# SwiGLU feed-forward on one core: a transposing load issued by ScalarE, half-chunk ups in the head, and seven casts placed behind the tail copies

## The chip, the core and the metric

The kernel runs on one core of a Trainium2 chip. The metric is the device time in microseconds of one execution; 116.36 us is the median of three runs of the kernel before. The engines are TensorE (PE in the profile; PEld is its weight load), VectorE (DVE), ScalarE (ACT), GpSimd (POOL) and SyncE (SP). SP does no arithmetic, it issues DMAs; ACT can issue DMAs too, on a queue of its own (the profile calls SP's queue q1 and ACT's q10). Each engine runs its own instructions in a fixed order and waits on semaphores.

## What is computed

```python
B, S, D, F = 1, 2048, 512, 1376          # bf16
g = silu(x @ w_gate)                     # [S, F]
u = x @ w_up                             # [S, F]
return (g * u) @ w_down                  # [S, D]
```

## The kernel before

**Tiling.** Tokens are cut into four chunks of 512 (c = 0 to 3), F into ten tiles of 128 (ft = 0 to 9) and a remainder of 96, D into four blocks of 128 (dk). x is kept transposed in `xT_sb` (D on the partitions), so that `w_sb` gives the stationary operand and x the moving one, and PSUM holds h transposed. PSUM has eight banks of 128x512 fp32.

**Two ways of multiplying.** Most of the gate and up work, and part of the down projection, is done two tiles by two chunks at a time with seven products in place of eight. VectorE and GpSimd form the sums of blocks that this needs (S1 to S4 and a cast A22 of the stationary side, T1 to T4 and a cast B22 of the moving side), PE multiplies them in fp32r. The rest, F tiles 0 to 5 of chunk 0 and some tiles of chunk 1, is done plainly: `classic` (L455) does a gate group and an up group of eight matmuls each (`gu_emit`, L406: for each dk two matmuls of 64 columns of F side by side), then ACT takes the silu and DVE multiplies (`classic_out`, L450). This plain work comes first, while weights and sums arrive.

**The order of the work.** Every operation is added to a `Plan` (L30) with the keys it reads and writes, an assumed duration, and a priority. PE and SP keep the order in which operations are added. For ACT, DVE and POOL `schedule` (L58) picks, by assumed times, whatever can start first, and by priority among equals (lower numbers first; the casts here have 9, the copies out of PSUM 0 to 2). The order so found is then fixed in the program. `after=` adds a dependency on given operations. So where an operation stands in the queue of ACT or DVE follows from assumed times, and when it runs follows from semaphores.

**Loads (L253 to L319).** All are issued by SP, in this order: `xn`, tokens 0 to 255 as they lie in memory (L282); `wg0`, gate weights of F tiles 0 and 1 (L289); `x0b`, tokens 256 to 511 by a transposing DMA (L290, issued at L279); `wu0`, up weights of F tiles 0 and 1 (L291); then weights `wg2`, `wu2`, `wg4`, `wu4` (L292), the transposing load `x1` of chunk 1 (L294), `wg6`, `wu6`, `wg8`, `wu8`, `wut`, `x2`, `x3`, the down weights `wd` and small pieces. Each weight load of two F tiles is 256 KB, `x0b` is 256 KB, each of `x1` to `x3` 512 KB.

**The head (L340 to L391, L670 to L680).** PE runs warming matmuls, then transposes tokens 0 to 255 itself; DVE and ACT copy the four dk blocks out of PSUM into `xT_sb` (`x0a`, L391; ACT has dk 1 and 3). On ACT stands ahead of these copies only a small silu of constants (L342), which makes it load its table. Then PE does F tiles 0 and 1 of chunk 0: gates on tokens 0 to 255 (sixteen matmuls of 256 columns), gates on tokens 256 to 511 (sixteen more, they need `x0b`), ups on all 512 tokens (sixteen matmuls of 512 columns, they need `wu0` and `x0b`).

**The start of the down projection (L933 to L980).** PE does plain output tiles (`body`, L699, into banks 4, 5, 0 and 1), and between them two blocks of `tails` (L711): the contribution of the 96 remaining F rows, in matmuls of 32 rows of which four run side by side. After the first block ACT copies banks 2, 3, 6 and 7 to `ts_sb` (`keep_tails`, L741); ACT also copies the finished output tiles to `o_sb` (`out_tile`, L693). After the second block ACT copies the same banks to `sg_sb`. Then come two seven-product units (`DownUnit`, L828): `a` with X, Y, W in banks 1, 3, 2 and `b` with 6, 3, 7. The first product of `a`, `p1` (L881, matmuls at L850), writes bank 1, so it must wait until `out_tile` of tile N3+1 has copied that bank. `keep` (L857, on DVE) reads bank 1 after each of `p1`, `p6` and `p7`.

`down_sums` (L756) adds the sums for those units: S1, S2 on POOL, T1 to T4, S3 and S4 on DVE, and on ACT seven casts (L818 to L821, issued from L527): two of 128x640 for A22 and five of 128x512 for B22, with priority 9 and behind T1 (`late`). A22 is read first by `a.p4` (L903), B22 by `a.p3` (L907).

Of the kernel before, what the change touches and what calls it, by code (L numbers as in the profile page):

```python
# [4 lines left out]
ACT = mybir.ActivationFunctionType  # L5
# [9 lines left out]
A_BUSY, A_LAG = 485, 180  # L15
# [152 lines left out]
def bass_standalone__swiglu_ffn__prompt_kernel(nc, x, w_gate, w_up, w_down, out):  # L168
    _, S, D = x.shape
    F = w_gate.shape[1]  # L170
    P = 128
# [26 lines left out]
    with ExitStack() as es:  # L198
# [53 lines left out]

        landed = 2700  # L253

        def load(name, emit, writes, busy, lag):
            nonlocal landed
            landed += lag
            i = take(homes[name] if name in homes else rest[0])
            plan.add("S", emit, writes=writes, busy=busy, lag=1800, dma=(i, 16)).land = landed + (2500 if landed > 10000 else 0)

        slabs = [(0, 2), (2, 4), (4, 6), (6, 8), (8, NFF + 1)]
        slab_of = {ft: a for a, b in slabs for ft in range(a, b)}
# [1 line left out]
        def load_w(name, src, m, c0, f0, f1):  # L264
            load(
                name,
                lambda e: e.dma_start(
                    w_sb[:, :, m, c0:c0 + f1 - f0], src[:, f0:f1].rearrange("(k p) f -> p k f", p=P)
                ),
                [name], 600, 3.2 * (f1 - f0),  # L270
            )
# [2 lines left out]
            load_w(f"wg{a}", w_gate, 0, a * P, a * P, min(b * P, F))  # L274
            load_w(f"wu{a}", w_up, 1, a * P, a * P, min(b * P, F - 32))

        def load_x(name, t0, t1):
            load(
                name, lambda e: e.dma_start_transpose(xT_sb[:, :, t0:t1], xf[t0:t1, :]), [name], 1500, 4.6 * (t1 - t0)  # L279
            )  # L280

        load(  # L282
            "xn",
            lambda e: e.dma_start(
# [1 line left out]
            ),  # L286
            ["xn"], 500, 770,
        )
        load_w("wg0", w_gate, 0, 0, 0, slabs[0][1] * P)  # L289
        load_x("x0b", HT, SC)  # L290
        load_w("wu0", w_up, 1, 0, 0, slabs[0][1] * P)  # L291
        for a, b in slabs[1:3]:  # L292
            load_slab(a, b)
        load_x("x1", SC, 2 * SC)  # L294
        for a, b in slabs[3:]:
            load_slab(a, b)
        load_w("wut", w_up, 0, F, F - 32, F)
# [41 lines left out]

        plan.add("G", lambda e: e.iota(diag[:, :], pattern=[[-1, P]], base=0, channel_multiplier=1), (), ["diag"], 300, 100, 0)  # L340
        plan.add("D", lambda e: e.tensor_single_scalar(ident[:, :], diag[:, :], 0.0, ALU.is_equal), ["diag"], ["ident"], 200, 100, 0)
        plan.add("A", lambda e: e.activation(adummy[:, 0:4], zero_c, ACT.Silu), (), ["adummy"], 1500, 100, 0)  # L342

        def pe(emit, reads, writes, n, step=PE_STEP, after=()):
            return plan.add("P", emit, reads, writes, int(n * step), PE_LAG, dma=None, after=after)
# [60 lines left out]
        def gu_emit(m, ft, c, b, dks, n0, n1):  # L406
            def emit(e):
                for dk in dks:
                    for h in (0, HC):
                        ins = e.matmul(  # L410
                            psum[h:h + HC, b, n0:n1], lhsT=w_sb[:, dk, m, ft * P + h:ft * P + h + HC],
                            rhs=xT_sb[:, dk, c * SC + n0:c * SC + n1], start=(dk == 0), stop=(dk == KD - 1),
                            tile_position=(0, h),
                        )
                return ins
            return emit
# [255 lines left out]
        for dk in range(KD):  # L672
            for ft, b in ((0, g0), (1, g1)):
                pe(gu_emit(0, ft, 0, b, [dk], 0, HT), [("x0a", dk), wkey[0]], [("b", b)], 0.5)
        for ft, b in ((0, g0), (1, g1)):
            pe(gu_emit(0, ft, 0, b, range(KD), HT, SC), ["x0b", wkey[0]], [("b", b)], 2)
        for ft, b in ((0, u0), (1, u1)):
            gu_group(1, ft, 0, b)
        classic_out(0, 0, g0, u0)
        classic_out(1, 0, g1, u1)  # L680

# [59 lines left out]
        def keep_tails(members, name, tiles):  # L741
            for c, (kind, i, b, start) in enumerate(members):
                if kind == "T":
                    t, k = ring(name, tiles)
                    tail_at[i, c] = t, k
                    copy_op("A", t, bank(b), [("b", b)], [k], 2)

        def before(keys):

# [6 lines left out]
        def down_sums(pool_after):  # L756

            flat = lambda s: ss_sb[:, s, :, :, :, :].rearrange("p n m k c -> p (n m k c)")
            NJ = NFF // 2
            HALF = NJ * 2 * P  # L760
            used = lambda s: before([("ss", s, n, m) for n in W_SUM.values() for m in range(2)] + [("ss", s, n, m) for n in W_SUM for m in range(2)])
            slots = {n: (slot_of[U_ORDER[1][1]], i) for i, n in enumerate(("S1", "S2"))}
            slots |= {n: (slot_of[U_ORDER[1][2]], i) for i, n in enumerate(("S3", "S4"))}
            slots["A22"] = slot_of[U_ORDER[1][4]], 0
            wview = wd_sb[:, :, :].rearrange("p (j a) (q e c) -> p a e j q c", a=2, e=2, c=P)
            hview_ = h0_sb[:, :, :].rearrange("p (j a) (c t) -> p a c j t", a=2, c=2)
            ds, dt = {}, {}
            for n, (s, i) in slots.items():
                ds[n] = flat(s)[:, i * HALF:(i + 1) * HALF].rearrange("p (j q c) -> p j q c", j=NJ, q=2)
            tt1 = tt_sb[1][:, :, :, :].rearrange("p n k c -> p (n k c)")  # L770
            tile = lambda a, i: a[:, i * NJ * SC:(i + 1) * NJ * SC].rearrange("p (j t) -> p j t", j=NJ)
            dt["T1"], dt["T2"], dt["T3"], dt["T4"] = tile(tt1, 0), tile(tt1, 1), th_sb[:, 0, :, :], th_sb[:, 1, :, :]
            dt["B22"] = tile(flat(slot_of[U_ORDER[1][3]]), 0)
            free = {"T1": before([("tt", 1, n, k) for n in X_SUM.values() for k in range(KH)])}
            free["T2"] = free["T1"]
            free["T3"] = free["T4"] = before([f"w{g}{a}" for g in "gu" for a, _ in slabs] + ["wut"])
            free["B22"] = used(slot_of[U_ORDER[1][3]])

            def s_sum(n, eng, after):
# [12 lines left out]

            def t_sum(n):
                for j0, j1 in ((0, 1), (3, 5), (1, 3)):
                    at = lambda n: dt[n][:, j0:j1, :]
                    rd = lambda n: at(n).bitcast(FP32)
                    B11, B12, B21, B22 = (hview_[:, k, c, j0:j1, :] for k in range(2) for c in range(2))
                    a, b, of_ = {
                        "T1": (B12, B11, ()), "T2": (B22, rd("T1"), ["T1"]),
                        "T3": (B22, B12, ()), "T4": (B21, rd("T2"), ["T2"]),  # L800
                    }[n]
                    t_ops[n] = tt_op(
                        "D", at(n), a, b, ALU.subtract,
                        [("h", ft, c) for ft in range(2 * j0, 2 * j1) for c in range(2)] + [("dt", o, j) for o in of_ for j in range(j0, j1)],
                        [("dt", n, j) for j in range(j0, j1)], 9, 1150 if j1 - j0 == 2 else D_BUSY, free[n],
                    )

            t_ops = {}
            s_sum("S1", "G", pool_after)
            s_sum("S2", "G", pool_after)  # L810
            t_sum("T1")
            t_sum("T2")
            t_sum("T3")
            s_sum("S3", "D", [t_ops["T3"]])
            t_sum("T4")
            s_sum("S4", "D", [t_ops["T4"]])
            late = [t_ops["T1"]]
            for q in range(2):  # L818
                cast_op("A", ds["A22"][:, :, q, :], wview[:, 1, 1, :, q, :], ["wd"], [("ds", "A22", q)], 9, 600, used(slots["A22"][0]) + late)
            for j in range(NJ):  # L820
                cast_op("A", dt["B22"][:, j, :], hview_[:, 1, 1, j, :], [("h", 2 * j + 1, 1)], [("dt", "B22", j)], 9, A_BUSY, free["B22"] + late)  # L821
            return ds, dt

        xflat = xT_sb[:, :, :].rearrange("p k t -> p (k t)")
        oT_sb = xflat[:, 0:KD * S // 2].rearrange("p (d c t) -> p d c t", d=KD, c=2)
# [104 lines left out]
            )  # L930
            copy_op("D", o_all[:, ob, c0:c1], psum[:, b, 0:c1 - c0], [("b", b)], [("o", t, c0)], 1)

        def down(ds, dt):  # L933
            N2, N3 = NST // 2, NST // 2 + TPC
            x_used = before([f"x{c}" for c in range(1, NSC)] + x_keys(0))
            for n0, n1 in ((0, NFF - 2), (NFF - 2, NFF)):
# [13 lines left out]
            first = [("T", 2, 2, True), ("T", 2, 3, True), ("N", N2 + 2, 4, True), ("N", N3 + 2, 5, True)]  # L950
            second = [("T", 3, 6, True), ("T", 3, 7, True), ("N", N2 + 3, 0, True)]
            tails([first, second])
            for members in (first, second):
                keep_tails(members, "sg", sg_sb)
            a = DownUnit(0, (1, 3, 2), ds, dt, x_used)
            b = DownUnit(1, (6, 3, 7), ds, dt, x_used)
            a.p1()
# [63 lines left out]
        for n in range(len(units)):  # L1021
# [12 lines left out]
            unit.p3()  # L1034
            unit.p4()
            unit = after
        ds, dt = down_sums(pool_last)
        down(ds, dt)

        plan.schedule()  # L1040
        plan.emit(engines, sems)
# [30 lines left out]
```

## Time and profile before

| | us |
|---|---|
| median of three runs (116.28 to 116.48) | 116.36 |
| the profiled execution | 116.42 |
| its span, first to last instruction | 115.1 |
| PE busy in the span | 111.0 |
| DVE, ACT, POOL busy | 76.4, 60.6, 59.9 |
| granted TensorE clock | 1.0 |

The profiled execution's own time is 1.3 us longer than its span: that is what lies around the instructions. All positions in time below are microseconds from the start of the span. Times of matmuls in the trace overlap, since their ends are modelled: the distance between starts is the rate.

### The profile page before, as it was taken

Reading aid. Unit: us, or ns where it says so; the run is one execution under the profiler, and the core shown is the slowest. Engines: PE = TensorE matmul, PEld = TensorE weight load, DVE = VectorE, ACT = ScalarE, POOL = GpSimd, SP = SyncE. Lnnn points to the kernel's source line nnn. Section 1 sums busy time; section 2 is a strip of 40 time slices with the busy share of each in tenths; the row PEclk is TensorE's granted clock in tenths of the full one; section 3 lists DMA queues with packets and bytes.
Section 4 is the critical chain, followed back from the end, with each engine's and each line's share of the span. In section 5 each row is a group of like instructions: output and inputs, shape, how many; then the busy total and the mean of one; then the engine's idle time right before and its main releaser. Section 6 shows DMA issues by size and latency. Waiting matters only on the chain.

```text
span 115.1 us, 1806 instructions
## 1 busy us (share of the span) xinstructions
PE 111.0 (96%) x662; PEld 66.9 (58%) x670; DVE 76.4 (66%) x112; ACT 60.6 (53%) x116; POOL 59.9 (52%) x75
## 2 busy tenths in 40 slices
PE   7989999999999999999999999999998999999993
PEld 2655555554567667685858676553443656866452
DVE  0113599766659394866849393799999977486423
ACT  5344276599756767878676767630799600000000
POOL 1475000599999999799999999980000000000000
DMA  3999899991000000000000000000022002327966
GB/s 95 261 292 252 216 282 267 251 354 31 0 0 0 0 3 3 0 6 0 3 0 0 0 0 0 6 0 0 0 91 80 11 0 46 51 46 181 200 193 201
DMA packets 22776, 9.84 MB, mean 86 GB/s; under 512 B 12816, under 2 KB 22640, under 8 KB 22768
## 3 DMA queue, kind: packets, MB, share of 16 engines
q1 hardware_dynamic: 20624, 8.69, 30.3%
q10 hardware_dynamic: 2144, 1.05, 3.2%
q8 instruction: 5, 0.08, 0.3%
q14 instruction: 3, 0.02, 0.1%
HBM read 4.75 MB, written 2.10 MB: 60 GB/s over the span
## 4 chain that ended last, share of the span: by engine, by line
PE 79%; DVE 7%; ACT 6%; DMA 3%; SPq 2%; issue 1%; DVEq 0%
PE psum L593 26%; PE psum L410 12%; PE psum L605 10%; PE psum L838 10%; PE psum L703 7%; PE psum L421 5%; PE psum L850 4%; DMA w_sb<-in_w_up_dram 3%; DVE tt_sb L336 3%; PE psum L474 3%; ACT ss_sb L527 3%; ACT o_sb L324 2%; ACT ts_sb L324 2%; PE psum L500 1%; SPq L279 1%; DVE h_sb L336 1%
## 5 line engine op out<-in xcount | busy, mean ns | idle before, releaser
L593 PE MATMUL psum<-tt_sb,ss_sb 128*128 128x512 f32 x140 | 35.3, 404 | 0.0
L593 PEld LDWEIGHTS psum<-tt_sb,ss_sb 128*128 128x128 f32 x140 | 26.3, 188 | 6.4
L336 DVE TENSOR_TENSOR ts_sb<-r_sb,psum 128x512 f32<-128x512 f32 x28 | 17.9, 682 | 12.4 <-ACT r_sb L324 12.4
L336 DVE TENSOR_TENSOR h_sb<-sg_sb,psum 128x512 bf16<-128x512 f32 x26 | 17.8, 683 | 8.6 <-PE psum L410 7.0
L331 ACT ACTIVATE sg_sb<-psum 128x512 f32<-128x512 f32 x26 | 15.5, 598 | 14.3 <-PE psum L410 7.8
L336 POOL TENSOR_TENSOR ss_sb<-w_sb 128x256 fp32r<-128x256 bf16 x20 | 13.1, 675 | 15.3 <-DVE tt_sb L336 11.1
L336 POOL TENSOR_TENSOR h_sb<-sg_sb,ts_sb 128x512 bf16<-128x512 f32 x14 | 18.4, 1314 | 1.7 <-ACT sg_sb L331 1.5
L703 PE MATMUL psum<-wd_sb,h_sb 128*128 128x512 bf16 (+2 forms) x97 | 18.0, 335 | 0.2
L324 ACT ACTIVATE r_sb<-psum 128x512 f32<-128x512 f32 x28 | 15.2, 595 | 5.7 <-PE psum L593 5.7
L410 PE MATMUL psum<-xT_sb,w_sb 128*64 128x512 bf16 (+1 forms) x160 | 16.1, 360 | 0.4 <-DMA w_sb<-in_w_up_dram 0.4
L703 PEld LDWEIGHTS psum<-wd_sb,h_sb 128*128 128x128 bf16 x100 | 8.3, 98 | 9.2 <-issue 1.0
L410 PEld LDWEIGHTS psum<-xT_sb,w_sb 128*64 128x64 bf16 x160 | 9.0, 111 | 7.3 <-DMA w_sb<-in_w_up_dram 0.7
L605 PE MATMUL psum<-xT_sb,w_sb 128*128 128x512 bf16 x52 | 12.6, 380 | 0.4 <-issue 0.2
L331 ACT ACTIVATE sg_sb<-ts_sb 128x512 f32<-128x512 f32 x14 | 8.9, 634 | 1.6 <-DVE ts_sb L336 1.6
L605 PEld LDWEIGHTS psum<-xT_sb,w_sb 128*128 128x128 bf16 x56 | 4.8, 98 | 7.0 <-issue 2.3
L336 POOL TENSOR_TENSOR ss_sb<-w_sb,ss_sb 128x256 fp32r<-128x256 bf16 x10 | 6.6, 683 | 0.0
L336 POOL TENSOR_TENSOR ss_sb<-ss_sb,w_sb 128x256 fp32r<-128x256 f32 x10 | 6.6, 676 | 0.0
L325 DVE CAST o_sb<-psum 128x512 bf16<-128x512 f32 (+2 forms) x6 | 2.9, 512 | 4.2 <-PE psum L703 3.1
L421 PE MATMUL psum<-xT_sb,w_sb 128*128 128x512 bf16 x24 | 5.7, 379 | 0.0
L838 PE MATMUL psum<-tt_sb,ss_sb 128*128 128x512 f32 x20 | 5.6, 417 | 0.0
L325 DVE COPY psum<-psum 128x512 f32<-128x512 f32 x7 | 4.9, 700 | 0.9 <-ACT sgy_sb L331 0.3
L838 PE MATMUL psum<-th_sb,ss_sb 128*128 128x512 f32 x20 | 5.5, 414 | 0.0
(71 smaller groups left out, 124.7 us busy)
## 6 DMA issues: line engine op xcount, KB each, us to landing
wd_sb<-in_w_down_dram SPq DMA_DIRECT2D x1, 1280.0 KB, 8.3
w_sb<-in_w_gate_dram SPq DMA_DIRECT2D x4, 256.0 KB, 4.2
w_sb<-in_w_up_dram SPq DMA_DIRECT2D x4, 256.0 KB, 4.4
out_dram<-o_sb SPq DMA_DIRECT2D x7, 128.0 KB, 1.8
out_dram<-xT_sb ACTq DMA_DIRECT2D x4, 128.0 KB, 2.4
out_dram<-xT_sb ACTq DMA_DIRECT2D x2, 256.0 KB, 3.3
w_sb<-in_w_gate_dram SPq DMA_DIRECT2D x1, 352.0 KB, 4.9
w_sb<-in_w_up_dram SPq DMA_DIRECT2D x1, 320.0 KB, 4.2
```

The lines of the kernel that those rows point to most:

```text
L324: return e.activation(out, src, ACT.Copy)
L325: return e.tensor_copy(out, src)
L331: "A", lambda e: e.activation(out, src, ACT.Silu), reads, writes, busy, A_LAG, prio
L336: engs, lambda e: e.tensor_tensor(out, a, b, alu), reads, writes, busy,
L410: ins = e.matmul(psum[h:h + HC, b, n0:n1], lhsT=w_sb[:, dk, m, ft * P + h:ft * P + h + HC], rhs=xT_sb[:, dk, c * SC + n0:c * SC + n1], sta ...
L421: ins = e.matmul(bank(b), lhsT=w_sb[:, dk, m, ft * P:(ft + 1) * P], rhs=xT_sb[:, dk, c * SC:(c + 1) * SC], start=(dk == 0), stop=(dk == KD ...
L474: ins = e.matmul(psum[m:m + HC, b, :], lhsT=w_sb[:, dk, 0, XC0 + m:XC0 + m + HC], rhs=xT_sb[:, dk, c * SC:(c + 1) * SC], start=(dk == 0), ...
L593: ins = e.matmul(bank(dst), lhsT=s[:, k, :], rhs=t[:, k, :], start=(start and k == 0), stop=(k == KH - 1), skip_group_check=True,)
L605: ins = e.matmul(bank(dst), lhsT=w_sb[:, k0 + k, m, f:f + P], rhs=xT_sb[:, k0 + k, c:c + SC], start=(start and k == 0), stop=(k == KH - 1) ...
L703: ins = e.matmul(psum[:, b, 0:c1 - c0], lhsT=hrows(F_ORDER[n], t, 0, P), rhs=wd_sb[:, F_ORDER[n], c0:c1], start=(start and n == n0), stop= ...
L838: ins = e.matmul(bank(dst), lhsT=self.ds[s][:, j, self.q, :], rhs=self.dt[t][:, j, :], start=(start and n == 0), stop=(n == NFF // 2 - 1), ...
L850: ins = e.matmul(bank(dst), lhsT=wd_sb[:, 2 * j + a, d * P:(d + 1) * P], rhs=h0_sb[:, 2 * j + a, 0:SC], start=(n == 0), stop=(n == NFF // ...
```

## The change

Three edits.

1. `load` and `load_x` take an engine and dependencies. `x0b` is issued by ACT, behind the silu of constants, which is added to the plan earlier now; `wg0` and `wu0` are issued one after the other by SP. `x1` stays on SP and waits for `x0b` to have landed.
2. In the head PE does after the gates on tokens 0 to 255 the ups on tokens 0 to 255 (sixteen matmuls of 256 columns), then gate 0, up 0, gate 1 and up 1 on tokens 256 to 511 (eight matmuls of 256 columns each).
3. The seven casts of A22 and B22 no longer follow T1. They follow the last `keep_tails` copies of either group after the second block of `tails`, and are added to the plan there.

```diff
-        def load(name, emit, writes, busy, lag):
+        def load(name, emit, writes, busy, lag, eng="S", after=()):
...
-            plan.add("S", emit, writes=writes, busy=busy, lag=1800, dma=(i, 16)).land = landed + (2500 if landed > 10000 else 0)
+            op = plan.add(eng, emit, writes=writes, busy=busy, lag=1800, dma=(i, 16), after=after)
+            op.land = landed + (2500 if landed > 10000 else 0)
+            return op
...
+        table = plan.add("A", lambda e: e.activation(adummy[:, 0:4], zero_c, ACT.Silu), (), ["adummy"], 1500, 100, 0)
...
-        load_w("wg0", w_gate, 0, 0, 0, slabs[0][1] * P)
-        load_x("x0b", HT, SC)
-        load_w("wu0", w_up, 1, 0, 0, slabs[0][1] * P)
+        load_slab(*slabs[0])
+        x0b = load_x("x0b", HT, SC, "A", [table])
         for a, b in slabs[1:3]:
             load_slab(a, b)
-        load_x("x1", SC, 2 * SC)
+        load_x("x1", SC, 2 * SC, "S", [x0b])
...
-        plan.add("A", lambda e: e.activation(adummy[:, 0:4], zero_c, ACT.Silu), (), ["adummy"], 1500, 100, 0)
...
-        for ft, b in ((0, g0), (1, g1)):
-            pe(gu_emit(0, ft, 0, b, range(KD), HT, SC), ["x0b", wkey[0]], [("b", b)], 2)
         for ft, b in ((0, u0), (1, u1)):
-            gu_group(1, ft, 0, b)
+            pe(gu_emit(1, ft, 0, b, range(KD), 0, HT), [("x0a", dk) for dk in range(KD)] + [wkey[1]], [("b", b)], 2)
+        for m, ft, b in ((0, 0, g0), (1, 0, u0), (0, 1, g1), (1, 1, u1)):
+            pe(gu_emit(m, ft, 0, b, range(KD), HT, SC), ["x0b", wkey[m]], [("b", b)], 2)
...
-                    copy_op("A", t, bank(b), [("b", b)], [k], 2)
+                    last = copy_op("A", t, bank(b), [("b", b)], [k], 2)
+            return last
...
-            late = [t_ops["T1"]]
-            for q in range(2):
-                cast_op("A", ds["A22"][:, :, q, :], wview[:, 1, 1, :, q, :], ["wd"], [("ds", "A22", q)], 9, 600, used(slots["A22"][0]) + late)
-            for j in range(NJ):
-                cast_op("A", dt["B22"][:, j, :], hview_[:, 1, 1, j, :], [("h", 2 * j + 1, 1)], [("dt", "B22", j)], 9, A_BUSY, free["B22"] + late)
-            return ds, dt
+            def casts(after):
+                for q in range(2):
+                    cast_op("A", ds["A22"][:, :, q, :], wview[:, 1, 1, :, q, :], ["wd"], [("ds", "A22", q)], 9, 600, used(slots["A22"][0]) + after)
+                for j in range(NJ):
+                    cast_op("A", dt["B22"][:, j, :], hview_[:, 1, 1, j, :], [("h", 2 * j + 1, 1)], [("dt", "B22", j)], 9, A_BUSY, free["B22"] + after)
+            return ds, dt, casts
...
-            for members in (first, second):
-                keep_tails(members, "sg", sg_sb)
+            casts([keep_tails(members, "sg", sg_sb) for members in (first, second)])
```

More of the change, by code (lines that the diff above doesn't have):

```diff
@@ L275, in load_slab, with load_x @@
             load_w(f"wu{a}", w_up, 1, a * P, a * P, min(b * P, F - 32))
-        def load_x(name, t0, t1):
-            load(
-                name, lambda e: e.dma_start_transpose(xT_sb[:, :, t0:t1], xf[t0:t1, :]), [name], 1500, 4.6 * (t1 - t0)
+        def load_x(name, t0, t1, eng="S", after=()):
+            return load(
+                name, lambda e: e.dma_start_transpose(xT_sb[:, :, t0:t1], xf[t0:t1, :]), [name], 1500, 4.6 * (t1 - t0), eng, after
             )
+        table = plan.add("A", lambda e: e.activation(adummy[:, 0:4], zero_c, ACT.Silu), (), ["adummy"], 1500, 100, 0)
         load(
@@ L931, in last_rest, with down @@
             copy_op("D", o_all[:, ob, c0:c1], psum[:, b, 0:c1 - c0], [("b", b)], [("o", t, c0)], 1)
-        def down(ds, dt):
+        def down(ds, dt, casts):
             N2, N3 = NST // 2, NST // 2 + TPC
@@ L1036, in bass_standalone__swiglu_ffn__prompt_kernel @@
             unit = after
-        ds, dt = down_sums(pool_last)
-        down(ds, dt)
+        down(*down_sums(pool_last))
         plan.schedule()
```

## The prediction

> **What bounds the kernel now.** I read the page first, then PE's waits, the chain of waits that ended last, and the timeline around the two places where PE waits.
>
> ```profile
> PE 111.0 (96%) x662; PEld 66.9 (58%) x670; DVE 76.4 (66%) x112; ACT 60.6 (53%) x116; POOL 59.9 (52%) x75
> ```
>
> PE is busy for 111.0 of 115.1 us. An edit that leaves PE's work alone can only win what PE idles, so PE's waits are the whole budget:
>
> ```profile
> PE psum L410 <- DMA w_sb<-in_w_up_dram: 0.4, 1, 0.4
> PE psum L850 <- ACT o_sb L324: 0.4, 1, 0.4
> ```
>
> These are the only waits of PE for something else than its own start and issue. The first is the head: PE has done its gates and waits for `wu0`. The second is the start of the down units: `a.p1` waits for ACT to have copied bank 1. The chain of waits names both:
>
> ```profile
> 3.05 3.97 DMA w_sb<-in_w_up_dram
> 7.02 0.04 issue
> 7.06 14.00 PE psum L410 x128
> ...
> 85.99 1.55 ACT ss_sb L527 x3
> 87.54 0.50 ACT o_sb L324
> 88.04 0.05 issue
> 88.08 1.25 PE psum L850 x5
> ...
> 90.52 0.66 PE psum L703 x3
> ```
>
> `wu0` is issued by SP at 3.05 and lands 3.97 us later; and at 86 to 88 three casts (L527) stand ahead of the copy of bank 1. Between the two PE waits for no other engine, and after 88.08 the chain is PE almost throughout. So I take it that time won in the head reaches the end, and time won at 88 too.
>
> **Tail: the casts.** The edit moves seven casts. In the timeline of ACT and PE:
>
> ```profile
> 81.22 1.36 ACT L527 ACTIVATE ss_sb<-wd_sb 128x640 fp32r<-128x640 bf16 x2 [4.62 <-DVE tt_sb L336]
> ...
> 85.83 1.71 ACT L527 ACTIVATE ss_sb<-h_sb 128x512 fp32r<-128x512 bf16 x3
> 87.39 0.64 ACT L324 ACTIVATE o_sb<-psum 128x512 bf16<-128x512 f32 x1
> 87.87 0.68 ACT L527 ACTIVATE ss_sb<-h_sb 128x512 fp32r<-128x512 bf16 x1
> 88.39 2.11 ACT L324 ACTIVATE sg_sb<-psum 128x512 f32<-128x512 f32 x4
> 90.30 0.72 ACT L527 ACTIVATE ss_sb<-h_sb 128x512 fp32r<-128x512 bf16 x1
> ```
>
> ```profile
> 81.43 0.37 PE L731 MATMUL psum<-hty_sb,wdt_sb 32*128 32x512 bf16 x1
> 81.74 4.49 PE L703 MATMUL psum<-wd_sb,h_sb 128*128 128x512 bf16 x19
> ...
> 87.11 0.38 PE L731 MATMUL psum<-hty_sb,wdt_sb 32*128 32x512 bf16 x1
> 87.33 0.38 PE L731 MATMUL psum<-hty_sb,wdt_sb 32*128 32x512 bf16 x2
> 88.08 1.25 PE L850 MATMUL psum<-h_sb,wd_sb 128*128 128x512 bf16 x5 [0.37 <-ACT o_sb L324]
> ```
>
> The body that fills bank 1 ends at 81.74 + 4.49 = 86.23. Without the casts ACT copies it at once, 0.64 us, until about 86.9, before PE is through with its tails. What then sets the start of `a.p1` is PE itself. How long PE needs from the last 32-row matmul to the next full one stands at the first block: 81.43 to 81.74, 0.31 us. Here it is 87.33 to 88.08, 0.75 us. **Gain 0.75 - 0.31 = 0.44 us.** Bounds: the 0.37 us of idle that the profile gives, and 0.75 less one round of such matmuls (87.11 to 87.33, 0.22), which is 0.53.
>
> Late next is `keep` on DVE, which reads bank 1 before `a.p6` may write it, and the casts themselves:
>
> ```profile
> 89.46 0.68 DVE L336 TENSOR_TENSOR r_sb<-psum,ts_sb 128x512 f32<-128x512 f32 x1
> ...
> 98.47 2.49 PE L838 MATMUL psum<-th_sb,ss_sb 128*128 128x512 f32 x10
> 100.80 1.30 PE L838 MATMUL psum<-ss_sb 128*128 128x512 f32 x5
> ```
>
> `keep` ends at 90.14. `a.p6` follows the body of three matmuls, which ends in the chain at 90.52 + 0.66 = 91.18; 0.44 earlier that is 90.74, so 0.6 us are left even if `keep` comes no sooner. The four copies to `sg_sb` (2.11 us) start at about 87.5, and the casts (1.36 + 1.71 + 0.68 + 0.72 = 4.47 us) follow at 89.6: A22 is complete near 91.0, B22 near 94.1. PE reads them at 98.0 and 100.4 in the new timing. Behind them ACT has only the issues of the down units' stores, which need those very products. So I cost the delay of the casts at nothing; without that cover it would be paid one to one.
>
> **Head: what is removed and added.** Here are the issues of the transposing loads `x0b` and `x1`, the time from issue to landing of all four such loads (from the view of `xT_sb`; the shortest is `x0b`, the longest `x1`), and what ACT does:
>
> ```profile
> 1.67 1.33 SPq L279 DMA_TRANSPOSE xT_sb<-in_x_dram  x1
> ...
> 6.19 4.06 SPq L279 DMA_TRANSPOSE xT_sb<-in_x_dram  x1
> ```
>
> ```profile
> DMA to landing us min/median/max: 3.8/4.6/7.5
> ```
>
> ```profile
> 2.02 0.20 ACT L342 ACTIVATE act_dummy<-const-float32-0.0 128x4 f32<-128x4 f32 x1
> 4.15 0.85 ACT L324 ACTIVATE xT_sb<-psum 128x256 bf16<-128x256 bf16 x2 [1.92 <-PE psum L372]
> ```
>
> PE's work stays the same: 128 matmuls of 512 columns take 14.00 us, 0.109 each, so sixteen take 1.75; sixteen of 256 columns take half, 0.88. The gates on 256 tokens now end where the second half of them began. Its start is worked out from the row that follows: the last of 32 starts at 6.34, two run side by side every 0.109 us, so all are through at 6.45 and the first half at 6.45 - 0.88 = 5.57.
>
> ```profile
> L410 PE MATMUL psum<-xT_sb,w_sb x32: 272/273/412, 4.6 to 6.3; 128*64 128x256 bf16 x32
> ```
>
> Before, the head's four groups end at 7.06 + 1.75 = 8.81. After, with u the landing of `wu0` and t that of `x0b` (0.04 us from landing to start, as in the chain), they end at
>
> max(max(5.57, u + 0.04) + 0.88, t + 0.04) + 1.75.
>
> *`wu0`.* SP issues it at 1.67 in place of 3.05. With the 3.97 us that it took, u = 5.64. Bounds: 7.02 (it comes no sooner) and 1.67 + 3.2 = 4.9, by the load of `wg0` (the DMA view on a window with this issue alone; the last number is us from issue to landing):
>
> ```profile
> w_sb<-in_w_gate_dram SPq DMA_DIRECT2D x1, 256.0 KB, 3.2
> ```
>
> With 5.64 the ups on 256 tokens end at 6.56.
>
> *`x0b`.* ACT can issue it at 2.02 + 0.20 + 0.06 = 2.28, 0.6 us later than SP did. Its 3.8 us would give t = 6.1, and nothing would wait for it. But it no longer stands in line ahead of `wu0`; it shares the DMA engines with SP's queue, which from 1.67 on is never empty. The trace shows such sharing once, when ACT's stores meet SP's transposes, in the window 108.25 to 108.75:
>
> ```profile
> q10 hardware_dynamic: 196, 0.10, 67.5%
> q1 hardware_dynamic: 194, 0.05, 48.2%
> ```
>
> The two queues take turns packet by packet, 390 per us each. `x0b` is 1024 packets of 256 bytes, 2.6 us at that rate. A transposing DMA that nothing disturbs (the first of the down units', 128 KB) lands after 2.4 us; at the rate of `x3` (1883 packets in the window 17.3 to 19.1) its 512 packets take 0.5, which leaves 1.9 us before and behind the packets. So t = 2.28 + 1.9 + 2.6 = 6.78. The transposing DMA of the same size that was caught in that sharing (the sixth of the down units') gives the same: 4.5 us, 2.28 + 4.5 = 6.78.
>
> ```profile
> xT_sb<-xT_sb SPq DMA_TRANSPOSE x1, 2.4
> ...
> q1 hardware_dynamic: 1883, 0.47, 115.8%
> ...
> xT_sb<-xT_sb SPq DMA_TRANSPOSE x1, 4.5
> ...
> xT_sb<-in_x_dram SPq DMA_TRANSPOSE x1, 5.1
> ```
>
> I take 6.78. The head ends at 6.82 + 1.75 = 8.57: **gain 0.24 us.** Bounds: t = 6.1 and u = 4.9 give 8.20, gain 0.61; the 5.1 us of `x2` (512 tokens) give t = 7.38, an end of 9.17 and a loss of 0.36.
>
> *Cover.* Behind `x0b` on ACT stand the copies at 4.15; an issue of 1.33 us from 2.28 ends at 3.61, so they aren't held. SP now waits at `x1` for t, 6.78 where it began at 6.19; behind it stand `wg6` to `wdl`. `x1` landed 7.5 us after its issue, at 13.7. If it and all behind it came 0.6 us later, 14.3, the first reader would still not have waited:
>
> ```profile
> 14.88 1.22 DVE L336 TENSOR_TENSOR tt_sb<-xT_sb 128x1024 fp32r<-128x1024 bf16 x1
> ```
>
> **The sum.** 116.42 - 0.44 - 0.24 = 115.74 against the profiled execution. That lies 0.06 above the median of 116.36, so **115.7 us**.
>
> **Rivals.** *The head is fully hidden:* the gain is 0.5 to 0.6, 115.3 to 115.4. For it: SP no longer spends 1.33 us of issue between `wg0` and `wu0`. Against it: the shared window above.
>
> *The head gains nothing:* the four loads that the head needs are the same bytes through the same DMA engines, and the last of them landed at 7.02. If the last still lands then, now `x0b`, the head ends at 7.06 + 1.75 = 8.81 as before: 116.36 - 0.44 = 115.92. For it speaks the page's DMA row, each digit the busy tenths of 2.9 us, eight or more from the second on:
>
> ```profile
> DMA  3999899991000000000000000000022002327966
> ```
>
> By the Trainium skill, page "DMA: Bandwidth & Descriptors", section "Issuing engines are not separate DMA queues", issuing from a second engine saves only the sequencer's time to issue. The equal counts of q1 and q10 above agree with that, and by that rule this rival is the outcome.
>
> *The tail's gain is given back:* `keep` or another DVE operation stands differently in its queue and holds `a.p6` by 0.44 us or more: 116.36 - 0.24 = 116.12. Against it: the 0.6 us of room.
>
> *Slower, ACT is held in the issue.* The issue of `x1` took 4.06 us, since its queue was full of earlier loads. If ACT's issue of `x0b` is held like that, the copies of dk 1 and 3, due at 4.15, start only at 2.28 + 4.06 = 6.34, and PE's gates come 2.19 us later. PE's own work ends the head at 5.57 + 0.88 + 1.75 = 8.20 at best; it would be 10.39, 1.58 after 8.81: 116.36 - 0.44 + 1.58 = 117.5. The copies are late from an issue of 1.87 us on, each us costs one, and from 1.87 + (8.81 + 0.44 + 0.23 - 8.20) = 3.15 us on the whole is slower by over 0.2%. Against it: ACT's queue is empty then, and SP's own `x0b` took 1.33.
>
> *It doesn't do what it says:* only the tail works and the head loses its bound of 0.36 us: 116.28.
>
> **Chances.** Forecast (115.5 to 115.8) 0.38; head hidden 0.17; head gains nothing (near 115.92) 0.22; tail given back 0.07; head loses 0.36 0.08; slower 0.08. A measurement of this kernel tells some 0.2%, 0.23 us, from no change. So faster is 0.38 + 0.17 + 0.22 = 0.77; within 0.2% 0.07 + 0.08 = 0.15; slower 0.08. The range reaches from both gains at their upper bounds, 116.36 - 0.53 - 0.61 = 115.2, to the head's loss beside the tail's lower bound, 116.36 + 0.36 - 0.37 = 116.35, rounded to 116.4.
>
> **What would show it.** Tail: the start of L850 comes about 0.31 us after the last L731 and names no ACT; the row of L527 on `h_sb` lies behind the four `sg_sb` copies and ends before 95. Head: `x0b` issued on ACT at about 2.3 for 1.3 us and landing at about 6.8; `wu0` landing near 5.6; the wait of PE at L410 then names `xT_sb` and is some 0.3 us; the 512-column matmuls of the next group start near 8.57. An `x0b` after 7.02, an ACT issue beyond 1.87 us of length, or new PE waits between 9 and 88 make it wrong.

## The result, and the profile after

The kernel after took 121.22 us at the median of four runs (119.4 to 121.78), the one before 116.42 in the same comparison (116.28 to 116.83). The ratio is 1.0314, 95% interval 1.023 to 1.0398: slower, where 115.7 was forecast. The interval rests on the runs at 119.4 and 120.96; the other two, the profiled one among them, count as disturbed, and the profile of another execution at 120.97 (the last experiment) reads the same.

The profiled execution took 121.49 us with a span of 120.2, 5.1 more than before. First the page: PE's row, the granted clock and the GB/s in 40 slices of 3.0 us.

```profile
PE 112.8 (94%) x678; PEld 68.8 (57%) x686; DVE 76.3 (63%) x112; ACT 61.2 (51%) x116; POOL 59.8 (50%) x75
...
PEclk9999599999999999999999999999999999999999
...
GB/s 91 217 178 210 118 295 292 247 293 233 30 0 0 0 0 0 5 5 0 0 3 0 0 0 0 0 5 0 0 87 44 44 0 49 44 44 147 193 194 208
```

The same last row of before, in slices of 2.9 us:

```profile
GB/s 95 261 292 252 216 282 267 251 354 31 0 0 0 0 3 3 0 6 0 3 0 0 0 0 0 6 0 0 0 91 80 11 0 46 51 46 181 200 193 201
```

PE's share falls from 96 to 94%. One slice, 12 to 15 us, has a granted clock of half. And from the third slice on, where before moved 292, 252 and 216 GB/s, the row shows 178, 210 and 118. Apart from the tail, what is new lies in the first 16 us. PE's waits, all of them:

```profile
PE psum L411 <- DMA xT_sb<-in_x_dram: 2.2, 1, 2.2
PE psum L411 <- DMA w_sb<-in_w_up_dram: 1.8, 1, 1.8
PE psum L350 <- PEq L1059: 0.8, 1, 0.8
PE psum L606 <- issue: 0.2, 1, 0.2
```

The wait of 0.4 for ACT (L850 then, L854 now) is gone, and two waits for the head's loads have come, 4.0 us in place of 0.4. The chain of waits that ended last, two pieces of it:

```profile
2.26 8.61 DMA xT_sb<-in_x_dram
...
10.91 15.70 PE psum L411 x144
```

Before, this stretch read 7.06 and 14.00 for 128 matmuls of 512 columns. What is left at 10.91 is as much work: 32 matmuls of 256 columns count as 16, and 112 of 512. So the head costs 10.91 - 7.06 = **3.85 us by the landing of `x0b`** and 15.70 - 14.00 = **1.70 us by the rate of PE behind it**. With the tail's 0.44 that is 116.42 + 3.85 + 1.70 - 0.44 = 121.53; measured was 121.49.

*The landings.* ACT's issue, and the issues of `wu0` and `x0b` with the us from issue to landing:

```profile
2.26 1.35 ACTq L281 DMA_TRANSPOSE xT_sb<-in_x_dram  x1
```

```profile
w_sb<-in_w_up_dram SPq DMA_DIRECT2D x1, 256.0 KB, 6.0
xT_sb<-in_x_dram ACTq DMA_TRANSPOSE x1, 8.6
```

The issue is on time and as long as expected. But `wu0` takes 6.0 us in place of 3.97, and `x0b` 8.6 in place of 3.8. Packets, bytes in MB and share by queue in the windows 4.75 to 5.25 and 6.5 to 7.5 (q1 is SP's, q10 ACT's):

```profile
q1 hardware_dynamic: 124, 0.06, 78.6%
q10 hardware_dynamic: 1, 0.00, 0.2%
```

```profile
q1 hardware_dynamic: 136, 0.07, 64.5%
q10 hardware_dynamic: 126, 0.03, 41.5%
```

At 5.25, 3.0 us after ACT began to issue, one packet of `x0b` has moved; it moved at 4.99. Most of this start is not new: in `e4_sp_holds` below, where `x0b` lands in time, its first packet moves at 4.52, also after an issue at 2.26. In the second window the queues do take turns, 136 to 126, but at 130 per us each where I had 390. The DMA engines aren't idle meanwhile. In the row of the window 5 to 7, which ends in DMA share and GB/s, they are busy and move 142 GB/s, where those of before move 243:

```profile
5.00:7.00 2.00, 0.85 (x14) 0.58 (x10) 0.00 (x0) 0.39 (x2) 0.77 (x2) 1.00 0.99 142
```

*PE's rate.* The matmuls of L411 in each us (count in brackets, then granted clock, DMA share, GB/s):

```profile
11.00:12.00 1.00, 1.00 (x20) 0.95 0.52 128
12.00:13.00 1.00, 1.00 (x14) 0.50 0.62 142
13.00:14.00 1.00, 1.00 (x10) 0.50 2.64 206
14.00:15.00 1.00, 1.00 (x8) 0.50 0.06 7
15.00:16.00 1.00, 1.00 (x10) 0.84 1.16 280
16.00:17.00 1.00, 1.00 (x14) 1.00 1.19 302
```

From 12 to 15 the clock is half, and the 0.95 and 0.84 at the edges put the stretch from 11.9 to 15.3: 3.4 us at half rate cost 1.7. No wait stands in it: PE has work and does it slowly. By the Trainium skill, page "TensorE: Matmul & The Clock Gate", section "Part 1: The HAM clock gate", an idle window of some 3.4 us halves the clock and a busy one of about that length restores it. The length agrees. But neither gap before it was that long: 1.83 and 2.17 us, with 1.06 us of work between.

*The tail.* PE and then ACT around the start of the down units:

```profile
92.87 0.38 PE L732 MATMUL psum<-hty_sb,wdt_sb 32*128 32x512 bf16 x2
93.18 1.25 PE L854 MATMUL psum<-h_sb,wd_sb 128*128 128x512 bf16 x5
```

```profile
93.08 2.07 ACT L326 ACTIVATE sg_sb<-psum 128x512 f32<-128x512 f32 x4 [0.69 <-PE psum L732]
95.18 1.37 ACT L528 ACTIVATE ss_sb<-wd_sb 128x640 fp32r<-128x640 bf16 x2
96.45 2.69 ACT L528 ACTIVATE ss_sb<-h_sb 128x512 fp32r<-128x512 bf16 x5
```

The first full matmul starts 0.31 us after the last of 32 rows, 0.75 before. The casts follow the copies and end at 99.14; less the 5.1 us by which everything is later, that is 94.0.

### The profile page after: what moved, and what is told of

The parts are those of the page before. It is cut to its first block, busy times and chain, and to the rows that moved or that the text cites. A ratio compares the mean times of both kernels' runs of the same rounds, so it can differ in the third digit from the quotient of the medians.

```text
span 120.2 us, 1839 instructions
## 1 busy us (share of the span) xinstructions
PE 112.8 (94%) x678; PEld 68.8 (57%) x686; DVE 76.3 (63%) x112; ACT 61.2 (51%) x116; POOL 59.8 (50%) x75
## 3 DMA queue, kind: packets, MB, share of 16 engines
HBM read 4.75 MB, written 2.10 MB: 57 GB/s over the span
## 4 chain that ended last, share of the span: by engine, by line
PE 88%; DMA 7%; ACT 1%; DVE 1%; issue 1%
PE psum L594 27%; PE psum L704 14%; PE psum L411 13%; PE psum L606 10%; PE psum L842 10%; DMA xT_sb<-in_x_dram 7%; PE psum L422 4%; PE psum L854 4%; PE psum L475 3%; PE psum L732 3%; PE psum L501 1%; ACT L284 1%; DVE o_sb L327 1%; ACT act_dummy L284 0%; PE psum L929 0%
## 5 line engine op out<-in xcount | busy, mean ns | idle before, releaser
L411 PE MATMUL psum<-xT_sb,w_sb 128*64 128x512 bf16 (+1 forms) x176 | 18.1, 370 | 4.0 <-DMA xT_sb<-in_x_dram 2.2
L411 PEld LDWEIGHTS psum<-xT_sb,w_sb 128*64 128x64 bf16 x176 | 10.7, 121 | 11.0 <-DMA xT_sb<-in_x_dram 2.4
```

What stands on the lines that cost most here:

```text
L411: ins = e.matmul(psum[h:h + HC, b, n0:n1], lhsT=w_sb[:, dk, m, ft * P + h:ft * P + h + HC], rhs=xT_sb[:, dk, c * SC + n0:c * SC + n1], sta ...
```

## The experiments

The theories, as the expectations name them. By the *two-queue* theory the loss comes from `x0b` being on ACT's queue beside SP's full one; one form of it lays it on the transposition there. By the *order* theory it comes from the order of loads and matmuls, whichever queue is used. By the *backlog* theory a load on ACT's queue waits for what SP has been given meanwhile. The times of single executions stand beside the before of the same chip: 116.5 for the first four, 116.63 for the next four, 116.72 for the three after them, 115.95 (itself a single execution) for the last two.

**The casts alone** (`e1_casts_only`), after with the head of before:

```diff
-        load_slab(*slabs[0])
-        x0b = load_x("x0b", HT, SC, "A", [table])
+        load_w("wg0", w_gate, 0, 0, 0, slabs[0][1] * P)
+        load_x("x0b", HT, SC)
+        load_w("wu0", w_up, 1, 0, 0, slabs[0][1] * P)
```

with `x1` free and the PE order of before. Expected:

> The kernel before with the third edit alone: the seven casts behind the copies to sg_sb, the head as it was. If the tail was priced rightly, a.p1 starts about 0.31 us after the last 32-row matmul, PE waits for ACT no more at that place, and the time is 0.44 us (0.37 to 0.53) under before, near 116.0 beside 116.4. If the tail gives it back later, the time equals before's.

Measured: 115.95, ratio 0.9951 (0.9927 to 0.9975), span 114.7. PE's waits, the only row:

```profile
PE psum L351 <- PEq L1060: 0.8, 1, 0.8
```

and PE at the start of the down units:

```profile
87.41 0.38 PE L733 MATMUL psum<-hty_sb,wdt_sb 32*128 32x512 bf16 x2
87.72 1.25 PE L855 MATMUL psum<-h_sb,wd_sb 128*128 128x512 bf16 x5
```

Again 0.31 us, and the span is 0.4 shorter. The tail's step is right, and the whole loss is the head's.

**`x0b` third on SP's queue** (`e2_x0b_sp_third`), all else as after:

```diff
-        x0b = load_x("x0b", HT, SC, "A", [table])
+        load_x("x0b", HT, SC)
...
-        load_x("x1", SC, 2 * SC, "S", [x0b])
+        load_x("x1", SC, 2 * SC)
```

> The changed kernel with x0b issued by SP, behind wu0; the ups first on 256 tokens and the late casts stay. Theory of the two queues (a transposing load in flight on one queue slows, and is slowed by, plain loads on the other, far beyond taking turns): with one queue nothing of that is left; wu0 lands near 5.5 to 6.0, x0b near 6.8 to 7.0, the head ends at 8.5 to 8.9, and the time is 115.4 to 116.0. Rival, the order of the work (ups first, or x0b behind wu0, is what costs): wu0 and x0b land late here as well, the head ends beyond 10, and the time is over 117.

Measured: 115.96, ratio 0.9955 (0.9935 to 0.9975), span 114.7. With the same order and one queue `wu0` lands at 5.24 and `x0b` at 6.16, and PE doesn't wait in the head. The order theory falls. But the time is that of the casts alone: the head's gain is given back at `x3`. PE is ready for it 0.75 us sooner than in the casts alone and starts on it 0.08 sooner.

```profile
PE psum L350 <- PEq L1059: 0.8, 1, 0.8
PE psum L475 <- DMA xT_sb<-in_x_dram: 0.5, 1, 0.5
```

The chain shows the issue of `x1` and the landing of `x3`:

```profile
5.87 5.42 SPq L281
...
18.19 6.13 DMA xT_sb<-in_x_dram
```

The issue of `x1` is held for 5.42 us (4.50 in the casts alone), which puts the issue of `x3` 0.46 later. The larger part is that `x3` takes 6.13 us to land, 4.60 in the casts alone. In the fifteen traces of this case `x3` takes 6.1 to 6.4 us in four (this one, `e4_sp_holds`, `e9_sp_holds_later`, `e10_p1_first`) and 4.1 to 4.8 in eleven. In those four, and in no other, a 16 KB instruction fetch (the profile's queue q8) begins while `x3` is in flight, here at 22.05. Whether the fetch is the cause was not tested.

**A plain load on ACT** (`e3_act_plain`): it leaves out the transposition of `x0b`, whose tokens 256 to 511 are then not transposed. With the kind of the load its packets change too, 512 of 512 bytes in place of 1024 of 256.

```diff
-        x0b = load_x("x0b", HT, SC, "A", [table])
+        x0b = load(
+            "x0b",
+            lambda e: e.dma_start(
+                xT_sb[:, :, HT:SC], xf[HT:SC, :].rearrange("(p j) (h t) -> p (j h) t", j=2, t=HT),
+            ),
+            ["x0b"], 1500, 4.6 * HT, "A", [table],
+        )
```

> The changed kernel with a plain load of the same 256 KB on ACT's queue in place of the transposing one; it leaves out the transposition of tokens 256 to 511, so that their values are in the wrong places. Theory of the two queues with a transposing load: without the transposition they only take turns, wu0 lands by 6.3 and x0b by 7.2, and the time is 115.5 to 116.2. Rival, the backlog (x0b and wu0 are late because two queues share with all of SP's waiting loads, whatever kind they are): wu0 lands after 7 and x0b after 8.5, and the time is over 117.5.

Measured: 117.12; `wu0` lands at 7.23, `x0b` at 7.85, PE waits 1.6 us for `wu0`. So `wu0` is nearly as late as in after (7.64) without any transposition on ACT's queue; the transposition, with its packets, accounts for 10.87 against 7.85 of `x0b` at most. Neither theory's numbers are met in full. And here the DMA engines don't slow down:

```profile
5.00:7.00 2.00, 0.70 (x14) 0.43 (x8) 0.00 (x0) 0.27 (x1) 0.87 (x2) 1.00 1.11 299
```

They move 299 GB/s where those of after move 142. So a plain load on ACT makes the others late by sharing a full rate, and the drop of the rate needs something more.

**SP holds its further loads until `x0b` has landed** (`e4_sp_holds`):

```diff
-        for a, b in slabs[1:3]:
-            load_slab(a, b)
+        load_w("wg2", w_gate, 0, 2 * P, 2 * P, 4 * P, [x0b])
+        load_w("wu2", w_up, 1, 2 * P, 2 * P, 4 * P)
+        load_slab(*slabs[2])
```

> The changed kernel with SP waiting for x0b to have landed before it issues wg2 and all behind it, so that only xn, wg0 and wu0 are in flight beside x0b. Theory of the two queues: x0b and wu0 are still in flight together, so wu0 lands after 6.5 and x0b after 7.5. Rival, the backlog: with no loads waiting, x0b lands by 6.5 and wu0 by 6. Either way wg2 now lands late, some 3 us after x0b, and PE waits for it, so the time itself is 117 or more; the landings are what counts.

Measured: 117.92. The landings are what the prediction wanted, `wu0` at 5.42 and `x0b` at 6.26:

```profile
w_sb<-in_w_up_dram SPq DMA_DIRECT2D x1, 256.0 KB, 3.8
xT_sb<-in_x_dram ACTq DMA_TRANSPOSE x1, 4.0
```

PE then does the head's 64 matmuls in one piece (its end is modelled):

```profile
4.70 3.68 PE L412 MATMUL psum<-xT_sb,w_sb 128*64 128x256 bf16 x64 [0.23 <-DVE xT_sb L328]
```

ACT's queue and the transposition are the same as in after, so neither by itself is the cause. The time is lost further on, since `wg2` and all behind it are issued 4 us later than in after (PE waits 1.0 for `wg2`, 0.6 for `wu2`, 0.5 for `x3`).

**PE kept busy in the two waits** (`e5_fill`), by 9 and 10 matmuls of constants into a free bank:

```diff
+        fill(9)
         for ft, b in ((0, u0), (1, u1)):
             pe(gu_emit(1, ft, 0, b, range(KD), 0, HT), ...)
+        fill(10)
```

> The changed kernel with matmuls of constants into a free bank in the two stretches of the head in which PE waits: nine before the ups on 256 tokens, ten before the second halves (0.216 us each). Theory of the clock (part of the loss is that PE, after waiting in the head, runs for about 3.5 us at half the rate): the half-rate stretch goes, the granted clock is 1.0 in every run, and the time is 119.4 to 119.8, 1.5 to 2 us under the changed kernel's 121.2, the landings of wu0 and x0b staying as late. Rival (the stretch of half rate has nothing to do with the waiting): the stretch stays and the time is 121 or more.

Measured: 120.19 (119.71 to 120.65), ratio 1.0318 (1.0275 to 1.0361). That misses the theory's 119.4 to 119.8, and it is not measurably below after's 1.0314. What the fill does to the rate is in the chain behind the second fill:

```profile
10.89 13.95 PE psum L411 x144
```

13.95 where after took 15.70 for the same matmuls, and the granted clock is 1.0 in all four executions, where it was below 1.0 in three of the four of after: with the gaps filled no half rate follows. That the time is no better is in part the fill's own doing: `x0b` landed at 9.85, and the fill, sized for 10.87, held PE until 10.89. And `wu0`, issued at 1.66 beside the same loads as in after, came here when I had predicted it, at 5.63:

```profile
w_sb<-in_w_up_dram SPq DMA_DIRECT2D x1, 256.0 KB, 4.0
```

So its delay is not there in every execution; that of `x0b` is in all three traces of these loads (10.87, 9.85 and, in the last experiment, 10.60).

**The new PE order with the loads of before** (`e6_pe_order`), issued as in the first experiment:

> The kernel before with the second and third edit: ups first on 256 tokens and late casts, and the loads as they were, x0b on SP between wg0 and wu0. Theory (the order on PE needs wu0 early and costs by itself): wu0 lands near 7.0 as before, PE waits for it from 5.6 on, 1.4 us, and then has 0.88 + 1.75 us to do: the head ends at 9.7, the time is 0.9 above the kernel with the late casts alone, near 116.8. Rival (the order on PE is harmless): the time is 116.0.

Measured: 116.62; `wu0` at 6.74, PE waits 1.1 us for it. The head ends at 9.43 where that of the casts alone ends at 8.91: the new order alone costs some 0.5 us, since each of its ups and the second halves behind them now stand behind `wu0`. With `wu0` at the 7.11 of the casts alone it would be 0.9, as expected.

**`wu0` on ACT, `x0b` second on SP, the PE order of before** (`e7_wu0_act`):

```diff
-        load_slab(*slabs[0])
-        x0b = load_x("x0b", HT, SC, "A", [table])
+        load_w("wg0", w_gate, 0, 0, 0, slabs[0][1] * P)
+        load_x("x0b", HT, SC)
+        load_w("wu0", w_up, 1, 0, 0, slabs[0][1] * P, "A", [table])
```

> The kernel before with the late casts and one load moved: wu0 is issued by ACT behind its table load, x0b stays on SP between wg0 and wg2. Theory of the backlog (a load on the second queue is late while SP's queue is full, and the load it is issued beside is held up too): wu0 lands after 7.0 though it is issued 0.75 us earlier than before, and x0b after 5.5. Rival (only a transposing load on ACT is late): wu0 lands by 6.3 and the head ends at 8.2 to 8.4.

Measured: 120.44. Now a plain load is on ACT and the transposing one on SP, and both are late:

```profile
w_sb<-in_w_up_dram ACTq DMA_DIRECT2D x1, 256.0 KB, 6.5
xT_sb<-in_x_dram SPq DMA_TRANSPOSE x1, 7.1
```

It isn't the transposing load on ACT alone that comes late, SP's loads do too. Even `wg0`, issued 1.06 us ahead of ACT's load, lands at 5.83, and PE waits 1.5 us for it; in after it landed at 4.40. From 5 to 7 the DMA engines move 133 GB/s, as few as in after, though the load on ACT is plain; the transposing one is on SP.

**Room for `x3` in the second version** (`e8_classic_first`, `e10_p1_first`). Two attempts to keep its head gain by work that needs `x3` later. The first does a plain group ahead of the remainder tiles of chunks 2 and 3 and the next one ahead of `p6`, the second the first product:

```diff
+        classic(1, early[-3:-2], [6, 7])
         plan_x(2, 4)
...
-        classic(1, early[-3:-2], [6, 7])
         for n in range(len(units)):
-            unit.p6()
             if n == 0:
                 classic(1, early[-2:-1], [2, 3])
+            unit.p6()
```

```diff
-        plan_x(2, 4)
-        plan_x(3, 5)
+        unit = make(0)
+        unit.p1()
+        plan_x(2, 6)
+        plan_x(3, 7)
         plan_y(1, 3)
         y_out(1, 3)
-        unit = make(0)
-        unit.p1()
```

> The kernel with x0b third on SP's queue, ups first on 256 tokens and late casts, and on PE a plain group of chunk 1 moved ahead of the remainder tiles of chunks 2 and 3 (and the next such group ahead of the first unit's second product), so that x3 is needed 1.7 us later. Theory (the head's 0.7 us were won and given back where PE waits for x3): that wait goes, the 0.5 to 0.7 us reach the end, 115.2 to 115.5. Rival (another wait takes its place at the start of the units): the time stays near 115.9 and PE's waits name another engine there.

> x0b third on SP's queue, ups first on 256 tokens, late casts, and on PE the first unit's first product moved ahead of the remainder tiles of chunks 2 and 3 (which take banks 6 and 7 in place of 4 and 5), so that x3 is needed 0.9 us later and the plain group still covers the end of the remainder tiles. Theory (the head's gain was given back at the wait for x3): the wait goes, 115.2 to 115.6. Rival (another wait takes its place): 115.9 or more, and PE's waits name it.

Both missed: 117.46, ratio 1.0071 (1.0048 to 1.0094), and 117.3, ratio 1.0049 (1.002 to 1.0078). The first has a wait of 0.6 us for `wu0` (6.05) and a new one for DVE, the second two of 0.5 us for DVE:

```profile
PE psum L422 <- DVE hl_sb L338: 1.1, 1, 1.1
```

In the second PE was also at half rate until 6.65, so that the head ended at 9.07 although `wu0` was there at 5.68; in the first it ended at 8.92. So in neither profiled execution was there a gain of the head left to keep (before 8.81). And in the second the chain still runs through `x3`, which lands at 25.36, and over ACT and DVE to one of those waits.

**Only `wg2` competes** (`e9_sp_holds_later`): as `e4_sp_holds`, but `wg2` goes out at once and the hold begins at `wu2`.

> The changed kernel with SP issuing wg2 behind wu0 and only then waiting for x0b: one load competes with x0b where the changed kernel has four. Theory of the backlog, by degrees (each load waiting on SP costs x0b its turns): x0b lands between the 6.3 us without any and the 10.9 of the changed kernel, near 7 to 7.5, and wu0 before 6.2. Rival (any load on SP issued after it is enough to trigger the whole loss): x0b lands after 8.5 and wu0 after 7.

Measured: 117.86; `wu0` 5.40, `x0b` 7.51.

```profile
xT_sb<-in_x_dram ACTq DMA_TRANSPOSE x1, 5.3
```

With none, one and four further loads given out by SP meanwhile, `x0b` takes 4.0, 5.3 and 8.6 us (with four 7.6 and 8.3 in the other two traces).

**`x0b` first of all** (`e12_x0b_first`), issued by ACT at 0.73, ahead of its table load:

```diff
+        x0b = load_x("x0b", HT, SC, "A")
         table = plan.add(...)
...
-        x0b = load_x("x0b", HT, SC, "A", [table])
```

> The changed kernel with x0b as ACT's first instruction, ahead of its table load, so issued at about 0.74, before wg0 and wu0. Theory (loads of the two queues are served about in the order of issue, and only what is issued into a full SP queue is held up): x0b lands by 5.5 and wu0 by 6.3; xn and wg0 come up to 1 us later than in the kernel before, since x0b goes first, and the head starts that much later; head end 8.3 to 9.3, time 115.5 to 116.5. Rival (an ACT load is held up whenever SP has loads waiting): x0b lands after 7.5 and the time is over 118.

Measured: 118.46; `x0b` 5.37, but `wg0` 5.20 and `wu0` 6.94. The landing of `x0b` is the theory's, the time the rival's. Packets by queue in the window 3.5 to 4.5:

```profile
q1 hardware_dynamic: 441, 0.23, 74.4%
q10 hardware_dynamic: 400, 0.10, 45.0%
```

Here the queues share at 441 and 400 packets a us, as in the prediction's window at 108: taking turns isn't slow by itself. The time goes to `wg0`, for which PE waits 1.1 us, to 0.6 for `wu0`, and to half rate again, in the chain:

```profile
6.98 16.56 PE psum L411 x160
```

These 160 matmuls are worth 48/2 + 112 = 136 of 512 columns, 14.88 us, so 1.68 are over.

**SP issues on as soon as ACT has issued** (`e13_sp_after_issue`): a small silu on ACT behind the issue of `x0b`, and `wg2` waits for that, not for the landing.

```diff
+        mark = plan.add("A", lambda e: e.activation(adummy[:, 4:8], zero_c, ACT.Silu), (), ["amark"], 100, 100, 1, after=[table])
-        for a, b in slabs[1:3]:
-            load_slab(a, b)
+        load_w("wg2", w_gate, 0, 2 * P, 2 * P, 4 * P, [mark])
+        load_w("wu2", w_up, 1, 2 * P, 2 * P, 4 * P)
+        load_slab(*slabs[2])
```

> The changed kernel with a second small silu on ACT behind the issue of x0b, and SP waiting for it before it issues wg2 and the rest: SP's four loads are then issued from about 4 us on, behind the whole issue of x0b, but in flight with it. Theory of the order of issue (a load on the second queue is served behind what the other queue was given before it, and with what is given during its issue; the queues don't disturb each other once started): wu0 lands by 5.6 and x0b by 6.6, nearly as with no loads waiting (5.4 and 6.3). Rival (loads of both queues in flight are what slows both): x0b lands after 7.5 and wu0 after 6.2.

Measured: 116.01 beside 115.95 for before. SP issues `wg2` at 3.89 and three more by 5.9, all while `x0b` is in flight, and still:

```profile
w_sb<-in_w_up_dram SPq DMA_DIRECT2D x1, 256.0 KB, 3.7
xT_sb<-in_x_dram ACTq DMA_TRANSPOSE x1, 4.0
```

`x0b` lands at 6.26, `wu0` at 5.37, and PE waits for no load any more, neither in the head nor for `x3`. So it is not enough for the loss that loads of both queues are in flight. Their packets hardly move side by side here, though; in the window 4.75 to 5.25 nearly all are ACT's:

```profile
q10 hardware_dynamic: 394, 0.10, 135.2%
q1 hardware_dynamic: 4, 0.00, 0.9%
```

What the run shows is that loads which SP issues behind ACT's issue don't hold `x0b`. The loss is found only where SP issues while ACT does. But 116.01 is not below 115.95, and the span of 114.7 is that of the casts alone; the reason stands in the rate (L413 is the line of these matmuls here):

```profile
4.70:5.70 1.00, 1.00 (x10) 1.00 1.33 243
5.70:6.70 1.00, 1.00 (x20) 1.00 1.12 277
6.70:7.70 1.00, 1.00 (x24) 1.00 1.09 278
```

```profile
4.68 16.44 PE psum L413 x176
```

176 matmuls are worth 64/2 + 112 = 144 of 512 columns, 15.75 us at full rate; 16.44 is 0.69 over. The count of the first us is less than half that of the third, with the same width of 256 columns, though the column of the clock says 1.00. In the casts alone PE starts as slowly, but there it waits for `wu0` anyway: its 14.00 us start at 7.16 and end at 21.16, here the end is 21.12.

**After once more** (`after_again`):

> The changed kernel once more, for the scatter of its landings: wu0 between 6.5 and 8 and x0b between 9.5 and 11.5, PE at half rate after its waits or not, time 119.4 to 121.8.

Measured: 120.97; `wu0` 7.94, `x0b` 10.60, waits of 2.3 and 0.7 us, and 15.47 us for the rest of the head:

```profile
2.26 8.34 DMA xT_sb<-in_x_dram
10.64 15.47 PE psum L411 x72
```

(The chain names 72 of the 144 matmuls here.) Delay and half rate are both there again.

## Why the prediction was wrong

- *The tail, 0.44 us:* right, in the gap of 0.31 us, in the place of the casts, in the room of `keep`, and in the span of the casts alone.
- *ACT's issue of 1.33 us from 2.28 and its copies:* right, 1.35 from 2.26. The rival of ACT held in the issue did not occur; the time was lost behind an issue that was on time.
- *`wu0` at 5.64:* wrong, 7.64, outside its bounds of 4.9 to 7.02 (7.94 and 5.63 in the other two traces of these loads). *`x0b` at 6.78:* wrong, 10.87, outside 6.1 to 7.38, and 10.60 and 9.85 in the other two. **This is the step that failed.** `wu0` was priced by a row in which SP alone issues, and `x0b` by a stretch at the end of the kernel in which each queue holds one or two loads; its rate, 390 packets a us for each queue, was taken over to the head. There the queues shared at full rate; in the head they take turns but move a third of it. With SP held until ACT has issued, my 5.64 and 6.78 would have been on the safe side: 5.37 and 6.26.
- *The formula of the head:* right as far as waits go. With the landings measured, max(max(5.57, 7.68) + 0.88, 10.91) + 1.75 = 12.66 against 8.81 before: the 3.85 us. In `e4_sp_holds`, with 5.42 and 6.26, it gives 8.20, and the last of the 64 matmuls starts at 8.11.
- *PE's rate:* a term that I did not have, 1.70 us here. Filling the gaps removes it. It need not be there in every execution: without it the sum is 119.83, and the fastest of the four runs, at a granted clock of 1.0, took 119.4; that run has no trace. I took 0.109 us a matmul as given after any wait, and the 5.57 as a constant; in several runs the first matmuls go at half rate until some point that is not the same in each execution (0.69 us in the second last experiment), and with the loads of before the wait for `wu0` hides that.
- *The rival "the head gains nothing":* by the Trainium skill, page "DMA: Bandwidth & Descriptors", section "Issuing engines are not separate DMA queues", a second issuing engine saves its issue time and no more. The traces bear out the shared turns, but not that nothing is lost: the same four loads are through at 7.02 before and at 10.87 after. That a second queue may cost was among my cases only as the bound of 0.36 us; the slower rival was put on ACT, where nothing happened.
- *The bound that time won in the head reaches the end:* wrong in the second version. There PE is ready for `x3` 0.75 us sooner and starts on it 0.08 us sooner.

What stays open is why the DMA engines move so few bytes. The drop is in four traces, 133 to 178 GB/s from 5 to 7 us: the three of these loads (after, `e5_fill`, the last experiment) and `e7_wu0_act`. In all four SP issues while ACT does, and a transposing load is in flight. It is not there with a plain load in place of the transposing one (`e3_act_plain`, 299), nor where SP's loads are issued behind ACT's (`e13_sp_after_issue`, 262), nor with one load issued beside it (`e9_sp_holds_later`, 233), nor where `x0b` is issued ahead of all else (`e12_x0b_first`, 298). These are one execution each but for the three, and no run shows where the packets are held.

The casts alone, 0.9951, and `x0b` third on SP's queue, 0.9955, beat both kernels; the half-chunk ups and ACT's issue added nothing that could be measured.

## What to carry to other kernels

A load that moves to a second queue is not priced by its duration on the first: look for a window in which both queues are being given several loads, and if there is none, let the upper bound be open. When a wait goes, ask what ran slowly under its cover: PE's start-up rate was free as long as a load was late, and became the bound when it was not. Read PE's rate from the counts of matmuls in equal windows, since a busy PE and a granted clock of 1.00 can both stand beside half the rate.

## What the runs showed that I had not expected

- Two gaps of 1.83 and 2.17 us with 1.06 us of work between them brought 3.4 us at half rate. By the Trainium skill, page "TensorE: Matmul & The Clock Gate", section "Why this matters for your kernels", it is gaps of over some 3 us that are to be avoided; in this execution two shorter ones were enough.
- Landings of the same loads scatter from execution to execution: with the same head, `x0b` third on SP's queue landed at 6.16, 7.11 and 6.75 us, and the head ended at 8.16, 8.92 and 9.07.
- An issue can be held for microseconds: that of `x1` took 3.76 us in `e13_sp_after_issue`, and 5.42, 5.00 and 3.93 in the three traces in which `x0b` stood ahead of it in the same queue (`e2_x0b_sp_third`, `e10_p1_first`, `e8_classic_first`).
